# The weights' integer additions and w_out's low-part subtractions, moved from GpSimd to VectorE in an attention and feed-forward kernel

## The chip, the cores and the metric

The kernel runs on one core of one Trainium2 chip. The metric is the device time of one execution in microseconds (us), as the median of several runs. A core has five engines that matter here, each with its own in-order queue of instructions: TensorE (PE in the profile; PEld is its loading of weights), VectorE (DVE), ScalarE (ACT), GpSimd (POOL) and SyncE (SP), which here issues all the transfers (DMA).

## The reference: what is computed

There are two parts. The first is an attention between 512 tokens and 32 state vectors for each of 8 batches and 8 heads of width 64. Both directions are read: tokens attend to the state, and the state attends to the tokens.

```
scores = x @ state^T / 8 ;  a  = softmax over the 32 state vectors ;  xread = a @ state
scores2 = state @ x^T / 8;  a2 = softmax over the 512 tokens       ;  sread = a2 @ x
```

The two results are joined to 8 x 544 = 4352 rows of width 512 (heads side by side). The second part is a feed-forward layer on these rows:

```
h = rows @ w_in      (512 -> 2048)
g = h - tanh(h)
out = g @ w_out      (2048 -> 512)
```

The two weights arrive in 64-bit floating point, the rest in 32-bit.

## The kernel before, in words

**Stages.** The output is made in nine chunks (`Chunk`): eight of 512 token rows, one per batch, and one of 256 rows for the state reads. A chunk runs over 16 hidden blocks `f` of 128 columns. For each block `hidden(f)` makes `h` in PSUM (`hps`), `finish` takes `h - tanh(h)` (`t`, line 383) and splits it in a high and a low part (`g`, lines 90 and 91), and `output(f)` adds three products per 128 rows (lines 413 to 415) into PSUM: high by high, high by low and low by high. The attention weights and the state are folded into `w_in` ahead: `m`, for each chunk and group of four blocks, is the state multiplied with `w_in`.

**Split.** `split(hi, lo, src, sub)` (lines 88 to 91) has ScalarE copy `src` into `hi`, rounded to the reduced 32-bit format that TensorE multiplies fast. Then `lo = src - hi` is made on VectorE, or on the engine given as `sub`.

**Weights.** There are 32 blocks of 128 x 512 in 64-bit form, 16 of each weight. `Weight.load` (line 109) brings one raw block to SBUF, into one of five buffers in turn; each buffer must be free before its next load. `Weight.steps` (lines 118 to 125) makes 32-bit floats of the raw words with integer operations. VectorE shifts and masks the high word (line 120) and puts in the sign and the top exponent bit (line 121). ScalarE makes the rounding increment `r` from the low word (line 123). An integer addition puts the increment on the float's bits (line 124). A block of `w_in` then goes back to DRAM as `wf` and into the state products. A block of `w_out` is converted to a `wor` buffer, of which there are two, and split by `convert_wout` (line 230) into `wo`, which stays in SBUF for all nine chunks.

**Order of the work.** The first steps, from the scores of batch 0 to its first two hidden blocks, follow an order written out by hand, `SEQ` (line 597). Each letter is a step (`a`, `b`, `r`, `p` are the four steps of a weight's conversion), and `keep_in_program_order` pins each step behind the one before on its engine. `firstDVE` is the last VectorE step of this sequence. `FILL` (line 603) says behind which VectorE step the first conversions outside the sequence are queued. All the rest is traced in the loop over chunks and blocks at line 645. There, lists of due steps (`D0`) say at which of the 16 x 9 steps a weight is converted, an attention unit advanced or a state product made. From that trace a planner sets the order of instructions on each engine, with costs of its own; each engine then runs its queue strictly in that order and waits on semaphores.

**Names and lines used below.** `w`: a converted block of `w_in`. `wor`, `wo`: a converted block of `w_out`, and its split parts. `r`: the increment. `m`, `mr`: state products split and raw. `wst`: split blocks of `w_in` for the state products of later batches (lines 178 and 179). `aT`: attention weights, split. `e`, `z`, `s`: softmax values. `sr`: state reads. `mps`, `hps`, `ops`, `sps`: PSUM tiles.

Of the kernel before, what the change touches and what calls it, by code (L numbers as in the profile page):

```python
# [32 lines left out]
def attention_ffn(ctx: ExitStack, tc: tile.TileContext, xT, xn, bd, bh, sp, sm, sl, win, wout, xout, sout):  # L33
# [10 lines left out]
    nc = tc.nc  # L44
# [23 lines left out]
    wo = cpool.tile([P, NFF, 2, DM], F32R, name="wo")  # L68
# [19 lines left out]
    def split(hi, lo, src, sub=None):  # L88

        nc.scalar.copy(hi, src)  # L90
        return (sub or nc.vector).tensor_sub(lo, src, hi)  # L91

    class Weight:
# [17 lines left out]
        def steps(self, dst):  # L111

            if self.src.dtype == F32:
                return [lambda: None] * 3 + [lambda: nc.gpsimd.tensor_copy(dst, self.raw)]
            low, high = self.raw[:, :, 0], self.raw[:, :, 1]
            u, i = dst.bitcast(U32), dst.bitcast(I32)
            r = pool.tile([P, 512], I32, tag="cr", name=f"{self.name}r", bufs=CB)
            return [

                lambda: nc.vector.tensor_scalar(u, high, 3, 0x3FFFFFFF, ALU.logical_shift_left, ALU.bitwise_and),  # L120
                lambda: nc.vector.scalar_tensor_tensor(u, high, 0xC0000000, u, ALU.bitwise_and, ALU.bitwise_or),  # L121

                lambda: nc.scalar.activation(r, low, AF.Copy, scale=2.0**-29),
                lambda: nc.gpsimd.tensor_add(i, i, r),
            ]

        def convert(self, dst):
# [99 lines left out]
    def convert_wout(f, part):  # L227
        w = pool.tile([P, 512], F32, tag="wor", name=f"wor{f}", bufs=RB)
        part.convert(w)
        split(wo[:, f, 0], wo[:, f, 1], w, nc.gpsimd)  # L230


    def attention(b, aT):
# [372 lines left out]
    with tc.issue_after(afters[FILL[0]]):  # L606
        convert_wout(0, wos[0])
    load(1)
    for p in range(2):
# [20 lines left out]
        wo=list(range(0, 15)),  # L630
# [14 lines left out]
    for i in range(B + 1):  # L645
        for f in range(NFF):
            st = 16 * i + f
            with tc.issue_after(first):
                for _ in range(D0["conv"].count(st)):
                    convert_win(*next(convs))  # L650
                    load(1)
                for _ in range(D0["wo"].count(st)):
                    x = next(wo_it)
                    convert_wout(x, wos[x])
                    load(1)
# [73 lines left out]
```

## Time and profile before

| | |
|---|---|
| median of 3 runs | 692.74 us (692.58 to 693.80) |
| the profiled execution | 692.26 us |
| its span, first to last instruction | 690.5 us |
| TensorE busy | 658.9 us (95%) |
| VectorE busy | 462.5 us (67%), 755 instructions |
| ScalarE busy | 378.4 us (55%), 663 instructions |
| GpSimd busy | 78.3 us (11%), 59 instructions |
| moved by DMA | 99.3 MB |

How to read the rows shown below. Times are in us from the start of the span unless marked ns. A group's row names the line, the engine, the operation, the tile written and the tiles read, the shape and the number of instructions; behind the first bar stand busy time in us and the mean of one in ns, behind the second the idle time of the engine just before them and what ended it. A row of single instructions begins with start and length. A wait's row has who waited for whom, the total in us, the number of times and the longest. The slices cut the span in 40 equal parts and give the busy share of each in tenths. VectorE and TensorE instructions in a row overlap slightly at their ends, so a duration is a little longer than the distance to the next start.

### The profile page before, as it was taken

Reading aid. Unit: us, or ns where it says so; the run is one execution under the profiler, and the core shown is the slowest. Engines: PE = TensorE matmul, PEld = TensorE weight load, DVE = VectorE, ACT = ScalarE, POOL = GpSimd, SP = SyncE. Lnnn points to the kernel's source line nnn. Section 1 sums busy time; section 2 is a strip of 40 time slices with the busy share of each in tenths; the row PEclk is TensorE's granted clock in tenths of the full one; section 3 lists DMA queues with packets and bytes.
Section 4 is the critical chain, followed back from the end, with each engine's and each line's share of the span. In section 5 each row is a group of like instructions: output and inputs, shape, how many; then the busy total and the mean of one; then the engine's idle time right before and its main releaser. Section 6 shows DMA issues by size and latency. Waiting matters only on the chain.

```text
span 690.5 us, 9315 instructions
## 1 busy us (share of the span) xinstructions
PE 658.9 (95%) x3386; PEld 520.4 (75%) x3386; DVE 462.5 (67%) x755; ACT 378.4 (55%) x663; POOL 78.3 (11%) x59
## 2 busy tenths in 40 slices
PE   5888996999999999999999999999999999999997
PEld 2455664788788887888788878887878788888896
DVE  5998899965597559556877568636864587434442
ACT  3876867566675665447656555634533354333342
POOL 3676656200000000000000000000000000000000
PEclk9999999999999999999999999999999999999999
DMA  8898763563554553355535522643251312001300
GB/s 289 292 302 289 228 252 118 173 224 97 148 187 144 170 163 123 101 145 152 188 122 180 156 96 92 210 155 126 71 175 31 123 60 91 32 6 46 133 31 30
DMA packets 46317, 99.30 MB, mean 144 GB/s; under 512 B 6208, under 2 KB 12096, under 8 KB 46272
## 3 DMA queue, kind: packets, MB, share of 16 engines
q1 hardware_dynamic: 46272, 98.72, 44.3%
q8 instruction: 26, 0.43, 0.3%
q14 instruction: 19, 0.16, 0.1%
HBM read 66.72 MB, written 31.98 MB: 143 GB/s over the span
## 4 chain that ended last, share of the span: by engine, by line
PE 82%; DVE 9%; ACT 4%; DMA 2%; issue 2%; POOL 1%; SPq 0%; ACTq 0%; POOLq 0%; DVEq 0%
PE ops L415 16%; PE ops L413 16%; PE ops L414 16%; PE hps L376 9%; PE hps L377 9%; PE hps L375 9%; PE mps L187 2%; DVE w L121 2%; PE sps L262 1%; PE rps L329 1%; PE mps L186 1%; PE pps L319 1%; DVE g L91 1%; DVE wor L120 1%; DMA wo4d<-in_wout 1%
## 5 line engine op out<-in xcount | busy, mean ns | idle before, releaser
L413 PE MATMUL ops<-wo,g 128*128 128x512 f32 x544 | 210.2, 396 | 5.1 <-ACT wo L90 3.2
L414 PE MATMUL ops<-wo,g 128*128 128x512 f32 x544 | 214.0, 393 | 0.5 <-POOL wo L91 0.5
L415 PE MATMUL ops<-wo,g 128*128 128x512 f32 x544 | 205.2, 391 | 0.0
L383 DVE TENSOR_TENSOR t<-hps,t 128x512 f32<-128x512 f32 (+1 forms) x142 | 93.1, 658 | 104.4 <-ACT t L383 103.4
L383 ACT ACTIVATE t<-hps 128x512 f32<-128x512 f32 (+1 forms) x142 | 81.2, 574 | 137.7 <-PE hps L377 137.0
L413 PEld LDWEIGHTS ops<-wo,g 128*128 128x128 f32 x544 | 102.3, 188 | 33.7 <-ACT wo L90 5.7
L90 ACT CAST g<-t 128x512 fp32r<-128x512 f32 (+1 forms) x142 | 84.6, 596 | 76.7 <-DVE t L383 69.1
L91 DVE TENSOR_TENSOR g<-t,g 128x512 fp32r<-128x512 f32 (+1 forms) x142 | 99.0, 698 | 40.1 <-ACT g L90 38.6
L415 PEld LDWEIGHTS ops<-wo,g 128*128 128x128 f32 x544 | 102.4, 189 | 23.7 <-issue 1.3
L414 PEld LDWEIGHTS ops<-wo,g 128*128 128x128 f32 x544 | 102.5, 188 | 23.4 <-POOL wo L91 1.4
L375 PE MATMUL hps<-aT,m 128*128 128x512 f32 x248 | 99.3, 401 | 3.6 <-ACT m L90 1.9
L377 PE MATMUL hps<-aT,m 128*128 128x512 f32 x248 | 97.3, 394 | 1.1 <-DVE m L91 1.1
L376 PE MATMUL hps<-aT,m 128*128 128x512 f32 x248 | 98.1, 395 | 0.0
L375 PEld LDWEIGHTS hps<-aT,m 128*128 128x128 f32 x248 | 47.2, 190 | 15.8 <-ACT m L90 3.2
L91 DVE TENSOR_TENSOR wst<-w,wst 64x512 fp32r<-64x512 f32 x64 | 47.0, 734 | 16.9 <-ACT wst L90 15.4
L377 PEld LDWEIGHTS hps<-aT,m 128*128 128x128 f32 x248 | 47.1, 190 | 12.6 <-DVE m L91 2.8
L376 PEld LDWEIGHTS hps<-aT,m 128*128 128x128 f32 x248 | 47.3, 191 | 10.7 <-issue 1.1
L91 DVE TENSOR_TENSOR m<-mr,m 128x1024 fp32r<-128x1024 f32 x31 | 40.9, 1321 | 10.8 <-ACT m L90 10.0
L188 ACT COPY st<-mps 128x512 f32<-128x512 f32 x64 | 36.6, 588 | 13.5 <-PE mps L187 12.8
L90 ACT CAST wst<-w 64x512 fp32r<-64x512 f32 x64 | 39.6, 619 | 2.3 <-issue 1.5
L90 ACT CAST m<-mr 128x1024 fp32r<-128x1024 f32 x31 | 32.3, 1042 | 4.8 <-DMA mr<-md 4.7
L91 POOL TENSOR_TENSOR wo<-wor,wo 128x512 fp32r<-128x512 f32 x16 | 25.2, 1581 | 4.9 <-ACT wo L90 4.8
(218 smaller groups left out, 642.3 us busy)
## 6 DMA issues: line engine op xcount, KB each, us to landing
md<-st SPq DMA_DIRECT2D x144, 128.0 KB, 2.2
mr<-md SPq DMA_DIRECT2D x28, 512.0 KB, 4.1
xT<-in_xT SPq DMA_DIRECT2D x16, 512.0 KB, 4.3
xn<-in_xn SPq DMA_DIRECT2D x16, 512.0 KB, 4.6
w<-wf SPq DMA_DIRECT2D x16, 512.0 KB, 4.6
out_x<-ob SPq DMA_DIRECT2D x32, 256.0 KB, 2.1
wn<-wf SPq DMA_DIRECT2D x8, 512.0 KB, 4.0
ml<-md SPq DMA_DIRECT2D x8, 512.0 KB, 3.6
```

Of the source, the lines that this page charges most:

```text
L90: nc.scalar.copy(hi, src)
L91: return (sub or nc.vector).tensor_sub(lo, src, hi)
L121: lambda: nc.vector.scalar_tensor_tensor(u, high, 0xC0000000, u, ALU.bitwise_and, ALU.bitwise_or),
L187: nc.tensor.matmul(ps, s[:, 0, h], t[:, e], start=(g == 1), stop=True)
L188: nc.scalar.copy(stage[:, e], ps)
L375: nc.tensor.matmul(ps, mhi[k][:, cols], ahi[:, k], start=(k == 0), stop=False)
L376: nc.tensor.matmul(ps, mhi[k][:, cols], alo[:, k], start=False, stop=False)
L377: nc.tensor.matmul(ps, mlo[k][:, cols], ahi[:, k], start=False, stop=(k == nk - 1))
L383: tanhs.append((nc.scalar.activation(t, ps, AF.Tanh).ins, nc.vector.tensor_sub(t, ps, t).ins))
L413: nc.tensor.matmul(o, g[:, 0, tok], wo[:, f, 0], start=(f == 0), stop=False)
L414: nc.tensor.matmul(o, g[:, 0, tok], wo[:, f, 1], start=False, stop=False)
L415: return nc.tensor.matmul(o, g[:, 1, tok], wo[:, f, 0], start=False, stop=(f == NFF - 1)).ins
```

## The change

Two edits. In `Weight.steps` the integer addition of the rounding increment is issued on VectorE instead of GpSimd, for all 32 weight blocks; this includes the four additions `p0` to `p3` of the hand-written sequence, which thereby become VectorE steps of it. In `convert_wout` the subtraction for the low part of `w_out` is issued on VectorE, the default of `split`, instead of GpSimd, for all 16 blocks. Both are traced at the same places as before; the planner sets the order anew. GpSimd keeps two subtractions of the first softmax (line 528), the two of `aT` for batch 0 (line 301), and the constants at the start.

```diff
                 lambda: nc.scalar.activation(r, low, AF.Copy, scale=2.0**-29),
-                lambda: nc.gpsimd.tensor_add(i, i, r),
+                lambda: nc.vector.tensor_add(i, i, r),
             ]
...
     def convert_wout(f, part):
         w = pool.tile([P, 512], F32, tag="wor", name=f"wor{f}", bufs=RB)
         part.convert(w)
-        split(wo[:, f, 0], wo[:, f, 1], w, nc.gpsimd)
+        split(wo[:, f, 0], wo[:, f, 1], w)
```

## The prediction

> **What bounds the kernel now.** I read three views in this order: the busy shares with the slices, a table of busy time over five stretches, and the chain of waits.
>
> ```profile
> PE 658.9 (95%) x3386; PEld 520.4 (75%) x3386; DVE 462.5 (67%) x755; ACT 378.4 (55%) x663; POOL 78.3 (11%) x59
> ...
> PE   5888996999999999999999999999999999999997
> ...
> DVE  5998899965597559556877568636864587434442
> ...
> POOL 3676656200000000000000000000000000000000
> ```
>
> GpSimd (POOL) works only in the first eight of forty slices, the first 138 us. The change can act directly only there. The stretches, whose columns are length, busy time and instructions of PE, PEld, DVE, ACT and POOL, clock, DMA share and GB/s:
>
> ```profile
> 9.00:52.00 43.00, 33.67 (x142) 21.78 (x141) 41.72 (x64) 31.59 (x58) 29.55 (x21) 0.96 0.93 300
> 52.00:122.00 70.00, 56.86 (x229) 38.52 (x228) 63.94 (x84) 48.71 (x84) 44.25 (x30) 0.98 0.63 219
> 122.00:138.00 16.00, 16.00 (x87) 12.74 (x88) 15.63 (x28) 9.44 (x17) 3.33 (x2) 0.89 0.57 178
> 138.00:690.50 552.50, 548.78 (x2927) 446.62 (x2925) 340.31 (x581) 286.82 (x503) 0.00 (x0) 1.00 0.38 119
> ```
>
> From 122 us TensorE is busy without a gap: what remains from there is TensorE's own work, and the change doesn't touch it. Before that TensorE idles, 9.3 us in the second stretch and 13.1 us in the third. So the time can move only by as much as the point where TensorE fills up moves. What decides that point is VectorE: busy 41.7 of 43 us and 63.9 of 70 us, the fullest engine in both. From 9 to 52 us the DMA engines are nearly full too (0.93), with the weights coming in. The chain of waits agrees: VectorE has 9% of it (62 us), second to TensorE, and GpSimd 1%, with pieces such as these (start, length, what):
>
> ```profile
> PE 82%; DVE 9%; ACT 4%; DMA 2%; issue 2%; POOL 1%; SPq 0%; ACTq 0%; POOLq 0%; DVEq 0%
> ...
> 80.94 1.30 POOL wor L124
> 82.24 1.71 POOL wo L91
> ...
> 110.78 1.68 POOL wor L124
> 112.46 2.23 POOL wo L91
> ```
>
> **The change, part by part.** Removed from GpSimd: 32 integer additions (line 124, one per 128x512 block of both weights) and 16 subtractions into `wo` (line 91). Added to VectorE: the same 48. No DMA, no ScalarE step and no matmul is added or dropped.
>
> *What they cost on VectorE.* No integer addition runs on VectorE in this trace. The nearest row is line 121, also two 32-bit integer inputs in SBUF:
>
> ```profile
> 50.24 0.68 DVE L121 SCALAR_TENSOR_TENSOR w<-w22d,w 128x512 uint32<-128x512 uint32 x1
> 50.84 0.68 DVE L121 SCALAR_TENSOR_TENSOR w<-w23d,w 128x512 uint32<-128x512 uint32 x1
> ...
> 53.65 0.41 DVE L120 TENSOR_SCALAR wor<-wo3d 128x512 uint32<-128x512 uint32 x1
> ...
> 58.30 1.67 DVE L121 SCALAR_TENSOR_TENSOR w<-w30d,w 128x512 uint32<-128x512 uint32 x1
> ```
>
> One lasts 0.68 us, but the next starts after 0.60 us, so 0.60 us is what one takes of a full queue: 48 x 0.60 = 28.8 us. The bounds are 0.60 us, if it overlaps its neighbours as here, and 0.69 us, if it never does; I take 0.60, because the queue is full.
>
> [...]
>
> *What they stop costing.* The last row above is the same operation as the first, but 1.67 us long. At that moment GpSimd was running:
>
> ```profile
> 57.93 1.48 POOL L91 TENSOR_TENSOR wo<-wor,wo 128x512 fp32r<-128x512 f32 x1
> 59.37 1.75 POOL L124 TENSOR_TENSOR wor<-wor,wo4r 128x512 int32<-128x512 int32 x1
> ```
>
> So a VectorE instruction with two inputs in SBUF (line 120 too) stands still while a GpSimd addition runs. Groups of VectorE show how much. First from 52 to 140 us, then after 140 us, where GpSimd does nothing (last columns: busy us, mean ns):
>
> ```profile
> L91 DVE TENSOR_TENSOR g<-t,g 128x512 fp32r<-128x512 f32 x13 | 13.6, 1049 | 1.9 <-ACT g L90 1.8
> L383 DVE TENSOR_TENSOR t<-hps,t 128x512 f32<-128x512 f32 x14 | 9.5, 685 | 1.6 <-ACT t L383 1.4
> L91 DVE TENSOR_TENSOR m<-mr,m 128x1024 fp32r<-128x1024 f32 x5 | 9.1, 1828 | 0.5 <-ACT m L90 0.5
> L91 DVE TENSOR_TENSOR wst<-w,wst 64x512 fp32r<-64x512 f32 x8 | 8.5, 1068 | 0.3
> L292 DVE TENSOR_TENSOR e<-e,z 128x512 f32<-128x512 f32 x2 | 2.1, 1063 | 0.0
> ```
>
> ```profile
> L91 DVE TENSOR_TENSOR wst<-w,wst 64x512 fp32r<-64x512 f32 x56 | 38.4, 686 | 16.7 <-ACT wst L90 15.4
> L91 DVE TENSOR_TENSOR m<-mr,m 128x1024 fp32r<-128x1024 f32 x26 | 31.8, 1223 | 10.4 <-ACT m L90 9.6 <-PE ops L413 0.2 <-PE mps L187 0.2
> ```
>
> Line 383, one of whose inputs lies in PSUM, keeps its 685 ns; the others are stretched. Lines 120 and 121, 0 to 52 us and 52 to 140 us, in that order for each line (VectorE busy, count):
>
> ```profile
> 0.00:52.00 52.00, 14.46 (x15) 0.97 0.91 295
> 52.00:140.00 88.00, 11.01 (x17) 0.96 0.62 214
> ```
>
> ```profile
> 0.00:52.00 52.00, 11.82 (x15) 0.97 0.91 295
> 52.00:140.00 88.00, 16.68 (x17) 0.96 0.62 214
> ```
>
> From 52 us on, the stretch above the undisturbed length is: line 120, 11.01 - 17 x 0.41 = 4.0; line 121, 16.68 - 17 x 0.68 = 5.1; `g`, 13 x (1.049 - 0.685) = 4.7; `m`, 5 x (1.828 - 1.223) = 3.0; `wst`, 8 x (1.068 - 0.686) = 3.1; `e`, 2 x (1.063 - 0.685) = 0.8. Sum 20.7 us. Of the 48 moved instructions 31 fall into this stretch (the GpSimd rows number 32 there, and one of them starts before it): 31 x 0.60 = 18.6 us. VectorE gains 2.1 us.
>
> Before 52 us: line 120, 14.46 - 15 x 0.41 = 8.3; line 121, 11.82 - 15 x 0.68 = 1.6; sum 9.9 us. The remaining 17 moved instructions cost 10.2 us. Four GpSimd subtractions stay there (two at line 528, two into `aT`) and keep part of the stretch. I cost this stretch at nothing: the two sums nearly cancel, and the DMA share of 0.93 would hide a small gain. If that cover is missing, it costs the difference of 0.3 us and 1.0 us (1.67 - 0.68) for each instruction that those four still stretch.
>
> *Waits that go and come.* VectorE now waits for GpSimd, and GpSimd for ScalarE:
>
> ```profile
> DVE g L91 <- ACT g L90: 1.8, 2, 1.1
> DVE wor L120 <- POOL wo L91: 1.8, 2, 1.2
> ...
> POOL wo L91 <- ACT wo L90: 4.8, 5, 2.4
> POOL wor L124 <- ACT wo5r L123: 4.3, 1, 4.3
> ```
>
> The wait for `wo` (a `wor` buffer not yet free) ends, since writer and reader are then one engine in order: -1.8 us. New on VectorE are the waits that GpSimd took alone: the addition needs ScalarE's `r`, the subtraction ScalarE's `wo` high part. Whatever is queued behind them waits as well: `t`, `g`, `m`, and behind those TensorE. The nearest row is `g`, with the same pattern of cast and subtraction: 1.8 us for 13. The 13 `wo` subtractions from 52 us on should cost as much, +1.8 us; the additions I cost at nothing, as `r` depends on the load alone and can be ready before line 121 is. Bounds: nothing, if the order places both late enough, and 4.8 + 4.3 = 9.1 us, all of what GpSimd waited.
>
> *The hand-written order.* Four additions (`p0` to `p3`) now stand in VectorE's own start sequence; each delays what follows it there by 0.60 us. `p3` becomes the last VectorE step there, and so the one behind which the second block of `w_in`'s next column group is queued: one 0.60 us step later. These are inside the 17 above.
>
> **Sum.** The profiled execution took 692.26 us around a span of 690.5, 0.5 us below the median of 692.74. 692.26 - 2.1 - 1.8 + 1.8 = 690.2 us.
>
> **The rivals.**
>
> *In-order waits (slower).* The planner sets VectorE's order from its own costs; where ScalarE is later than planned, VectorE stands still with everything behind it. For: ScalarE is busy 48.7 of 70 us, and GpSimd's long waits were for it. Against: VectorE waits for ScalarE for only 3.7 us there today (`g` 1.8, `t` 1.4, `m` 0.5 in the groups). At the bound: 692.3 - 2.1 - 1.8 + 9.1 = 697.5 us. It decides from 3.9 us of new waits on; up to there they are paid for.
>
> *Nothing moves.* DMA and ScalarE set the pace as soon as VectorE eases: 692.3 us. For: 0.93 DMA share early. Against: 0.63 from 52 us on.
>
> *Shorter path.* The pieces of GpSimd in the chain, 1.30 + 1.71 + 1.68 + 2.23 = 6.9 us, become 4 x 0.60 = 2.4 and no wait comes new: a further -4.5 us, with the 2.1 of VectorE 685.7 us. Against: behind VectorE's queue the steps start later than on an idle GpSimd.
>
> *Pure load (slower).* If the stretching had another cause than GpSimd, 18.6 us would be added to a full VectorE after 52 us: 692.3 + 18.6 = 710.9 us. Against: the rows at 50 and 58 us. [...]
>
> **How the numbers follow.** What this kernel's measurement can tell from no change is about 0.2%, 1.4 us. The forecast gets 0.48, and its own range is 688.4 (no new waits) to 693.0 us (0.69 for each of 31: +2.8); of that 0.37 lies below 690.9 us and 0.11 within 0.2%. In-order waits 0.32, nothing moves 0.08, shorter path 0.09, pure load 0.03. Faster 0.37 + 0.09 = 0.46; same 0.11 + 0.08 = 0.19; slower 0.32 + 0.03 = 0.35. The range runs from just under the shorter path, 685.0, to the bound of the waits, 697.5; pure load and what little lies outside are left out.
>
> **What would show it.** Right: lines 120, 121, `g`, `m` and `wst` before 140 us at 0.41, 0.68, 0.69, 1.22 and 0.69 us; line 124 on VectorE at 0.68 with 0.60 from start to start; TensorE full a few us before 122. Wrong: VectorE idle before 122 us that grew by over 4 us with ScalarE as releaser (in-order waits), an unmoved 52 to 122 stretch with less busy VectorE (nothing moves), or stretched rows beside an idle GpSimd (pure load). A difference that arises after 138 us would be none of these, and would mean that the planner's order changed there.

## The result, and the profile after

The changed kernel takes 688.78 us (median of 6 runs, 687.84 to 690.70), the kernel before beside it 693.44 us. The ratio is 0.9939 with a 95% interval from 0.9922 to 0.9956: by the ratio 4.2 us faster (the two medians lie 4.7 us apart). The forecast was 690.2 us, 2.1 us faster than the profiled execution, with a range of its own from 688.4 to 693.0 us. So the direction was right, the forecast gain was half of the measured one, and 688.78 us lies just inside the lower end of that range. The profiled execution took 688.88 us around a span of 687.1 us, against 692.26 around 690.5: 3.4 us less.

The changed kernel's busy times, slices and, last, its chain of waits:

```profile
PE 660.5 (96%) x3386; PEld 521.7 (76%) x3386; DVE 458.2 (67%) x803; ACT 377.9 (55%) x663; POOL 6.6 (1%) x11
...
PE   4788988999999999999999999999999999999997
...
DVE  5897999965695559556876568546853587434442
...
POOL 2100000000000000000000000000000000000000
...
PE 85%; DMA 6%; DVE 4%; ACT 3%; issue 1%; SPq 0%; ACTq 0%; DVEq 0%
```

VectorE has 48 instructions more (803 against 755) and is busy 4.3 us less (458.2 against 462.5). GpSimd's part fell from 78.3 to 6.6 us. In the chain of waits VectorE's share fell from 9% to 4%, and DMA's rose from 2% to 6%. The table of stretches for the changed kernel, with the same columns as before:

```profile
9.00:52.00 43.00, 31.81 (x126) 19.21 (x126) 38.95 (x78) 28.92 (x54) 5.43 (x4) 0.92 0.89 289
52.00:122.00 70.00, 63.42 (x248) 44.87 (x249) 64.75 (x119) 52.11 (x90) 0.00 (x0) 0.93 0.68 235
122.00:138.00 16.00, 16.00 (x95) 13.11 (x95) 15.47 (x30) 11.87 (x22) 0.00 (x0) 1.00 0.63 198
```

TensorE's idle time from 52 to 122 us fell from 13.1 to 6.6 us, while from 9 to 52 us it rose from 9.3 to 11.2 us. Over the whole span it fell by 5.0 us, from 31.6 to 26.6 us, while TensorE's busy time rose by 1.6 us (its mean granted clock was 0.988, against 0.993 before): 3.4 us in all. Its last pause before it fills up ended at 121.9 us before, behind a VectorE queue, and ends at 112.2 us now (single TensorE instructions, first of the kernel before, then of the changed one):

```profile
121.88 0.65 PE L186 MATMUL mps<-wst,sms 128*128 128x512 f32 x1 [3.64 <-DVE sr L335]
```

```profile
112.19 0.80 PE L414 MATMUL ops<-wo,g 128*128 128x512 f32 x1 [1.27 <-DVE wo L91]
```

In the profile of a second execution of the changed kernel (`e6_both_again` below) the last pause of over 1 us ends at 114.1 us, and two short ones of 0.45 and 0.48 us follow, at 123.1 and 138.3 us.

The stretched groups are back at their undisturbed lengths. From 52 to 140 us in the changed kernel:

```profile
L91 DVE TENSOR_TENSOR g<-t,g 128x512 fp32r<-128x512 f32 x14 | 9.6, 685 | 0.1
L91 DVE TENSOR_TENSOR wo<-wor,wo 128x512 fp32r<-128x512 f32 x13 | 8.9, 684 | 0.1
L91 DVE TENSOR_TENSOR m<-mr,m 128x1024 fp32r<-128x1024 f32 x6 | 7.3, 1214 | 0.0
L91 DVE TENSOR_TENSOR wst<-w,wst 64x512 fp32r<-64x512 f32 x8 | 5.5, 687 | 0.3
```

`g` fell from 1049 to 685 ns, `m` from 1828 to 1214, `wst` from 1068 to 687. The added integer additions, and one of the line-121 instructions beside them:

```profile
34.52 0.69 DVE L124 CUSTOM_DVE_ANT_0 w<-w,w11r 128x1024 uint16<-128x1024 uint16 x1
35.12 0.68 DVE L124 CUSTOM_DVE_ANT_0 w<-w,w10r 128x1024 uint16<-128x1024 uint16 x1
35.72 0.69 DVE L121 SCALAR_TENSOR_TENSOR wor<-wo1d,wor 128x512 uint32<-128x512 uint32 x1
```

They last 0.68 to 0.69 us and follow each other after 0.60 us, as costed. What VectorE waits for from 52 to 122 us has changed:

```profile
DVE wor L120 <- DMA wo4d<-in_wout: 1.1, 1, 1.1
DVE w L120 <- DMA w31d<-in_win: 1.1, 1, 1.1
DVE w L120 <- PE mps L149: 1.0, 1, 1.0
DVE z L289 <- ACT e L282: 0.8, 1, 0.8
DVE wor L120 <- DMA wo5d<-in_wout: 0.6, 1, 0.6
DVE w L120 <- DMA wf<-w: 0.3, 1, 0.3
```

It now waits for loads (2.8 us here) and for a block's way back to DRAM (0.3 us). It doesn't wait for ScalarE before any `wo` subtraction.

### The profile page after: what moved, and what is told of

Same layout as the page of the kernel before. It is cut to its first block, busy times and chain, and to the rows that moved or that the text cites. A ratio compares the mean times of both kernels' runs of the same rounds, so it can differ in the third digit from the quotient of the medians.

```text
span 687.1 us, 9286 instructions
## 1 busy us (share of the span) xinstructions
PE 660.5 (96%) x3386; PEld 521.7 (76%) x3386; DVE 458.2 (67%) x803; ACT 377.9 (55%) x663; POOL 6.6 (1%) x11
## 4 chain that ended last, share of the span: by engine, by line
PE 85%; DMA 6%; DVE 4%; ACT 3%; issue 1%; SPq 0%; ACTq 0%; DVEq 0%
PE ops L413 17%; PE ops L414 17%; PE ops L415 17%; PE hps L376 9%; PE hps L377 9%; PE hps L375 9%; PE mps L187 2%; PE sps L262 1%; PE rps L329 1%; DMA mr<-md 1%; PE mps L186 1%; DMA w01d<-in_win 1%; DMA wf<-w 1%; PE pps L319 1%; DMA w31d<-in_win 1%; DMA wo1d<-in_wout 1%
## 5 line engine op out<-in xcount | busy, mean ns | idle before, releaser
L91 DVE TENSOR_TENSOR g<-t,g 128x512 fp32r<-128x512 f32 (+1 forms) x142 | 93.3, 657 | 42.4 <-ACT g L90 41.1
L377 PEld LDWEIGHTS hps<-aT,m 128*128 128x128 f32 x248 | 46.7, 188 | 11.0 <-DVE m L91 1.0
L91 DVE TENSOR_TENSOR wst<-w,wst 64x512 fp32r<-64x512 f32 x64 | 43.9, 686 | 16.4 <-ACT wst L90 15.0
L375 PEld LDWEIGHTS hps<-aT,m 128*128 128x128 f32 x248 | 46.6, 188 | 10.5 <-issue 0.7
L376 PEld LDWEIGHTS hps<-aT,m 128*128 128x128 f32 x248 | 46.7, 188 | 10.0 <-issue 0.5
L91 DVE TENSOR_TENSOR m<-mr,m 128x1024 fp32r<-128x1024 f32 x31 | 37.8, 1220 | 9.3 <-ACT m L90 8.6
L188 ACT COPY st<-mps 128x512 f32<-128x512 f32 x64 | 36.7, 587 | 12.3 <-PE mps L187 12.0
L187 PE MATMUL mps<-wst,sms 128*128 128x512 f32 x64 | 24.7, 394 | 0.0
```

Source lines behind the costliest of these rows:

```text
L187: nc.tensor.matmul(ps, s[:, 0, h], t[:, e], start=(g == 1), stop=True)
L188: nc.scalar.copy(stage[:, e], ps)
L375: nc.tensor.matmul(ps, mhi[k][:, cols], ahi[:, k], start=(k == 0), stop=False)
L376: nc.tensor.matmul(ps, mhi[k][:, cols], alo[:, k], start=False, stop=False)
L377: nc.tensor.matmul(ps, mlo[k][:, cols], ahi[:, k], start=False, stop=(k == nk - 1))
```

## The experiments

Three theories were to be told apart. Relief: GpSimd instructions hold up VectorE's, VectorE sets the pace until TensorE fills up, and the gain is the stretch removed less the work added. Path: the way from a load to a ready block got shorter. Order: the planner's new order made the gain.

**Parts of the change.** `e1_adds_only` moves the 32 additions alone, `e2_subs_only` the 16 subtractions alone.

```diff
 e1_adds_only, against the changed kernel
-        split(wo[:, f, 0], wo[:, f, 1], w)
+        split(wo[:, f, 0], wo[:, f, 1], w, nc.gpsimd)
 e2_subs_only, against the changed kernel
-                lambda: nc.vector.tensor_add(i, i, r),
+                lambda: nc.gpsimd.tensor_add(i, i, r),
```

> Only the 32 integer additions move to VectorE; the 16 w_out subtractions stay on GpSimd. Relief (a GpSimd instruction that reads SBUF holds up VectorE's two-input and line-120 instructions, and the gain is that stretch minus the load): two thirds of the whole change, VectorE's total busy time falls by about 3 us and the time to about 690.5 us. Path (the gain is the shorter way from load to wo, whatever VectorE's stretch): the additions stand in all 32 conversions, the subtractions only in 16, so again about two thirds, but VectorE's busy time plays no part. Order (the planner's new order makes the gain): no rule, anything from 687 to 694 us.

> Only the 16 w_out subtractions move to VectorE; the 32 additions stay on GpSimd. Relief: one third of the whole change, VectorE's total busy time falls by about 1.5 us, the time to about 692 us. Path: the subtraction is the last step before TensorE can use a block, and GpSimd took 1.28 to 2.25 us for it against 0.68 us, so it should give at least half of the whole, 691 us or less. Order: anything from 687 to 694 us.

`e1_adds_only`: 688.44 us, ratio 0.9939 (0.9922 to 0.9956), VectorE busy 459.9 us. `e2_subs_only`: 687.17 us, ratio 0.9915 (0.9902 to 0.9928), VectorE busy 458.5 us. The expectation of two thirds and one third fell: each part alone gives as much as both together, or more. VectorE's totals show part of why. The additions alone take 2.6 us off VectorE (462.5 to 459.9; about 3 was expected), the subtractions alone 4.0 us (to 458.5; about 1.5 was expected), and both together only 4.3 us (to 458.2). So the parts don't add: on top of the subtractions the additions take 0.3 us, on top of the additions the subtractions take 1.7 us. In time each part alone gained more than it took off VectorE, 4.5 us for 2.6 and 5.8 us for 4.0; this pair doesn't explain that.

**Contention alone.** `e3_idle_pool_work` gives GpSimd 48 additions back that nobody waits for. All other engines have the same instructions in the same order as in the changed kernel.

```diff
         split(wo[:, f, 0], wo[:, f, 1], w)
+        for _ in range(3):
+            nc.gpsimd.tensor_add(spare, wo[:, f, 0].bitcast(F32), wo[:, f, 0].bitcast(F32))
```

> The changed kernel with 48 more 128x512 additions on GpSimd (three per w_out block, each reading the block's high part twice, written to a spare tile that nobody reads). No other engine waits for them, and the order of every other engine is that of the changed kernel, so only contention can act. Relief: lines 120 and 121, the additions, g, m, wst and the wo subtractions on VectorE stretch again to 1.2 to 1.8 us where they meet one, 48 times about 0.7 us or some 30 us on an engine that is already full from 22 to 122 us, and the time rises by 10 to 30 us, to 699 to 719 us. Path and order: 688.8 us as before, nothing but GpSimd busy.

Measured: 711.10 us, ratio 1.0262 (1.0249 to 1.0275), so 22.3 us more than the changed kernel. VectorE's busy time rose by 27.6 us to 485.8 us. Its groups from 52 to 140 us, and the added GpSimd group (line 92 is line 91 of the other kernels, since a line was added):

```profile
L92 DVE TENSOR_TENSOR wo<-wor,wo 128x512 fp32r<-128x512 f32 x11 | 11.5, 1042 | 0.0
L92 DVE TENSOR_TENSOR g<-t,g 128x512 fp32r<-128x512 f32 x10 | 9.4, 940 | 0.0
L386 DVE TENSOR_TENSOR t<-hps,t 128x512 f32<-128x512 f32 x12 | 8.2, 681 | 0.1
```

```profile
L233 POOL TENSOR_TENSOR spare<-wo 128x512 f32<-128x512 f32 x48 | 65.6, 1367 | 75.7 <-ACT wo L91 73.2
```

The instructions with two inputs in SBUF are stretched again, and `t`, with one input in PSUM, is not. Path and order can't act here, so the contention is shown, and its price in this run: 0.58 us of VectorE for each GpSimd addition (27.6 us for 48).

**Does VectorE set the pace?** `e4_no_adds` drops the additions from the changed kernel.

```diff
-                lambda: nc.vector.tensor_add(i, i, r),
+                lambda: None,
```

> The changed kernel without the 32 integer additions (the weights miss the rounding increment of their low word; ScalarE still makes it). It takes 32 x 0.60 = 19.2 us from VectorE between 12 and 135 us and nothing from elsewhere. If VectorE sets the pace before TensorE fills up (the prediction's reading): 3 to 10 us less than the changed kernel, 679 to 686 us, bounded by TensorE's 13 us of idle time between 22 and 122 us. If the loads or ScalarE take over as soon as VectorE eases: 688 us, with VectorE idle for about 19 us more.

Measured: 674.54 us, ratio 0.9737 (0.9725 to 0.9750), 14.2 us less than the changed kernel, more than the upper end expected. VectorE's busy time fell by 18.4 us to 439.8 us, so each us off VectorE was worth 0.77 us. The run also prices the additions on either engine. With them on VectorE its total is 18.4 us higher (458.2), with them on GpSimd 18.7 us higher (458.5, `e2_subs_only`). With the subtractions on VectorE it is the same for VectorE whether it makes an addition itself or is held up by one. TensorE's busy time fell by 8.1 us too; the last section says what that may be.

**Once more side by side, and two variants.** `e6_both_again` is the changed kernel, `e7_subs_again` is `e2_subs_only`, both unaltered. `e5_no_pool` also moves the last four GpSimd subtractions. `e8_same_fill` queues one conversion behind the same VectorE step as before the change.

```diff
 e5_no_pool, against the changed kernel
-    P0 = json.loads('[0, 0, 0, 0, 1]')
+    P0 = json.loads('[0, 0, 0, 0, 0]')
-    SEQ = 'S0 c0 T0 S1 D D M0 c1 q0 a0 ... M1 b0 q1 E1 ...'
+    SEQ = 'S0 c0 T0 S1 D D M0 c1 B0 a0 ... M1 b0 B1 E1 ...'
 e8_same_fill, against the changed kernel
-    afters = [firstDVE[0], tanhs[0][1], tanhs[1][1]]
+    afters = [tanhs[1][1], tanhs[0][1], tanhs[1][1]]
```

> The changed kernel once more, beside the next three on one chip. Theory after the first four runs: up to about 122 us the time follows VectorE's busy time, about 0.8 us for each us (48 GpSimd additions that held it up for 27.6 us cost 22 us; 19.2 us less work on it gave 14 us), and the planner's order adds a few us either way. Expected 688 to 689 us.

> Only the 16 subtractions on VectorE, beside the changed kernel. VectorE's busy total was 458.5 us in that run against 458.2 us with both parts moved, so by VectorE's time the two are equal within 0.3 us; any difference beyond about 1 us is then the order or the path. Theory (the additions cost VectorE on either engine about the same): 687 to 689 us, within 1.5 us of the changed kernel. Rival (the first run's 687.2 against 688.8 was a real advantage of leaving the additions on GpSimd): 1 to 2 us below the changed kernel again.

> The changed kernel with the last four GpSimd subtractions (two of the first softmax at line 528, two into aT for batch 0) on VectorE as well: GpSimd only sets constants. By VectorE's time: 4 x 0.60 = 2.4 us more work, against some 2 us of stretch that ends: 0 to 1 us either way, 688 to 690 us. By the path: the first softmax is the start of everything, and its two subtractions take 0.68 us instead of 1.18 and 1.42 us, 0.5 to 1 us sooner: 687.5 us. If the order decides: 686 to 691 us.

> The changed kernel, but the second block of w_in's next column group queues behind the same VectorE step as before the change (the second hidden block's subtraction), not behind the addition p3 that has become the last step of the hand-written start. This undoes the one side effect of the change on the traced order. If that queueing matters by itself: up to 0.6 us less. Otherwise it is a measure of what a small change of the planner's input does: 687 to 691 us, with nothing that VectorE's total would explain.

| | VectorE busy, us | median, us | ratio (95% interval) |
|---|---|---|---|
| `e6_both_again` | 458.7 | 689.50 | 0.9943 (0.9924 to 0.9962) |
| `e7_subs_again` | 458.4 | 687.06 | 0.9915 (0.9899 to 0.9931) |
| `e5_no_pool` | 457.8 | 686.33 | 0.9900 (0.9883 to 0.9917) |
| `e8_same_fill` | 457.9 | 688.50 | 0.9931 (0.9916 to 0.9947) |

The advantage of leaving the additions on GpSimd came again, 2.4 us here and 1.6 us in the first pair, with VectorE totals 0.3 us apart. The intervals of the two ratios overlap a little, so I call it likely, and its cause open. `e5_no_pool` is the fastest kernel that computes everything, 6.6 us below the kernel before (692.95 us beside it). It lies 3.2 us below the changed kernel beside it, more than the expectation by VectorE's time (688 to 690 us) or by the path (687.5 us) gave. VectorE's total is only 0.9 us lower. Only the range named for the order, 686 to 691 us, holds it; the cause of the rest is open. The changed place in the order (`e8_same_fill`) makes no difference that can be told from none.

**Early, late, and writes without reads.** `e11_early_work` and `e12_late_work` put 21 idle GpSimd additions into the changed kernel, early or late. `e9_pool_writes` puts in 48 fills that write and don't read. TensorE, VectorE and ScalarE keep the order of the changed kernel in all three.

```diff
 e11_early_work, against e3_idle_pool_work
-        for _ in range(3):
+        for _ in range(7 if f < 3 else 0):
 e12_late_work, against e3_idle_pool_work
-        for _ in range(3):
+        for _ in range(3 if f >= 9 else 0):
 e9_pool_writes, against the changed kernel
+        for _ in range(3):
+            nc.gpsimd.tensor_copy(spare[:, 0:1], wo[:, f, 0, 0:1].bitcast(F32))
+            nc.gpsimd.memset(spare, 0.0)
```

> The changed kernel with 21 extra GpSimd additions that nobody waits for, seven behind each of the w_out blocks 0 to 2, so between about 31 and 58 us; every other engine keeps its order. They should hold up VectorE for some 12 us (48 of them did for 27.6 us). If the transfers set the pace before 52 us, as the prediction had it when it costed that stretch at nothing: under 3 us more than the changed kernel, below 692 us. If VectorE sets the pace there too: about 0.8 us for each, some 9 us more, 697 to 699 us.

> The same with 21 extra GpSimd additions, three behind each of the w_out blocks 9 to 15, so between about 102 and 140 us. If VectorE sets the pace up to the point where TensorE fills up: about 9 us more than the changed kernel, 696 to 699 us. If TensorE has work enough of its own by then: under 3 us more.

> The changed kernel with 48 GpSimd fills (constant 0.0 into a spare tile of 128x1280, three behind each w_out block, each behind a one-element copy), which write but don't read; every other engine keeps its order. If it is GpSimd's reading that collides with VectorE's second input: the two-input instructions (line 121, the additions, g, m, wst, wo) keep 0.68 us (m 1.22), only line 120, which reads and writes fast, may stretch, VectorE's total grows by less than 8 us, the time to 689 to 695 us. If any GpSimd work does: as with the 48 additions, VectorE's total up by over 20 us, and 705 to 711 us.

`e11_early_work`: 701.13 us, ratio 1.0115 (1.0095 to 1.0134), VectorE 471.5 us. That is 13.3 us more on VectorE and 12.3 us more time. `e12_late_work`: 701.94 us, ratio 1.0135 (1.0112 to 1.0158), VectorE 473.2 us: 15.0 us more on it, 13.2 us more time. Both are 2 to 6 us above the times expected; the additions held up VectorE for more than the 12 us assumed. In `e11_early_work` 12 of the 21 additions start before 52 us, the others up to 64 us (shortest, median and longest in ns, then the first and the last start in us):

```profile
L233 POOL TENSOR_TENSOR spare<-wo x21: 1038/1367/2639, 30.2 to 64.0; 128x512 f32<-128x512 f32 x21
```

An estimate: at 13.3 / 21 = 0.63 us each, the 12 early ones are 7.6 us of the stretch and the others 5.7 us. If the transfers hid the early part, the time could have risen by 5.7 us at most; it rose by 12.3 us. So VectorE sets the pace before 52 us as well as after; the transfers don't hide it. The share of the DMA engines from 9 to 52 us fell with it, from 0.89 in the changed kernel to 0.79: there the transfers wait for VectorE, at least in part.

`e9_pool_writes`: 691.66 us, ratio 0.9985 (0.9972 to 0.9999), VectorE 464.6 us. That is 6.4 us more on VectorE than in the changed kernel and 2.9 us more time, less for each us than in the other runs. Its VectorE groups from 52 to 140 us (line 92 is line 91 before, and line 121 is line 120):

```profile
L92 DVE TENSOR_TENSOR wo<-wor,wo 128x512 fp32r<-128x512 f32 x13 | 8.9, 683 | 0.1
L92 DVE TENSOR_TENSOR g<-t,g 128x512 fp32r<-128x512 f32 x13 | 8.9, 682 | 0.1
...
L121 DVE TENSOR_SCALAR w<-w33d 128x512 uint32<-128x512 uint32 x1 | 1.5, 1470 | 0.0
```

```profile
L234 POOL MEMSET spare<- 128x1280 f32 x48 | 57.2, 1191 | 2.9
```

GpSimd is nearly as busy as with the additions (57.2 us of fills against 65.6 us of additions), but from 52 us on the two-input instructions keep their 0.68 us: `wo` takes 683 and `g` 682 ns here, 1042 and 940 ns beside the additions of `e3_idle_pool_work`. The shift-and-mask of line 120 alone is stretched there: 12.71 us for 19 of them, 0.67 us each, against 6.85 us for 17, 0.40 us each, in the changed kernel. So in these two runs the additions, which read SBUF, stretched the two-input instructions, and the fills, which only write, did not. Why the fills stretch line 120, which has one input, no row says.

**A version that might beat all.** `e10_pool_adds_only` has the additions on GpSimd and all subtractions on VectorE.

```diff
 e10_pool_adds_only, against e5_no_pool
-                lambda: nc.vector.tensor_add(i, i, r),
+                lambda: nc.gpsimd.tensor_add(i, i, r),
```

> A version that might beat all: the 32 additions stay on GpSimd, every subtraction goes to VectorE (the 16 of w_out, two of the first softmax, two into aT). If the additions cost VectorE the same on either engine and the four early subtractions gave the 3 us that lie between the run without GpSimd work and the changed kernel: 685 to 687 us. If they gave it only because GpSimd then had nothing at all to do: 687 to 689 us.

Measured: 693.92 us, ratio 1.0014 (1.0002 to 1.0027): no faster than the kernel before, and both expectations missed. VectorE's total is 464.0 us, 5.6 us above `e7_subs_again`. Four moved subtractions account for 2.4 us of that; the rest is stretch from another meeting of the two engines' queues. The profile has it after 52 us: from there to 140 us line 121 takes 16.13 us for 19 instructions (12.26 us for 17 in `e7_subs_again`) and a subtraction of `m` 1.63 us (1.21 us). TensorE waits 5.5 us for `wo` subtractions on VectorE, 1.4 us in `e7_subs_again`. Why the planner's order came out so wasn't tried.

All different kernels together, by VectorE's busy time (where a kernel was measured twice, its first measurement):

| | VectorE busy, us | median, us |
|---|---|---|
| `e4_no_adds` | 439.8 | 674.54 |
| `e5_no_pool` | 457.8 | 686.33 |
| `e8_same_fill` | 457.9 | 688.50 |
| the changed kernel | 458.2 | 688.78 |
| `e2_subs_only` | 458.5 | 687.17 |
| `e1_adds_only` | 459.9 | 688.44 |
| before | 462.5 | 692.96 |
| `e10_pool_adds_only` | 464.0 | 693.92 |
| `e9_pool_writes` | 464.6 | 691.66 |
| `e11_early_work` | 471.5 | 701.13 |
| `e12_late_work` | 473.2 | 701.94 |
| `e3_idle_pool_work` | 485.8 | 711.10 |

From the first row to the last it is 36.6 us for 46.0 us, 0.80 us for each us of VectorE. The rows lie within about 2.6 us of that line. In the runs where only GpSimd's idle work differs, VectorE's part is shown to be the cause. What puts a kernel 2 to 3 us off the line stays open: a new order is the obvious candidate, but `e9_pool_writes`, whose order is unchanged, lies 2.6 us below it too. For the change itself this means: its 4.3 us of VectorE are worth 3.4 us by the line, and the measured 4.2 us can't be told from that, nor from 2 us more or less by path or order. No run has the changed work in the old order.

## Why the prediction was right, and where it was not

*What bounds the kernel*: right about VectorE; `e3_idle_pool_work` and `e4_no_adds` show that the time follows it in both directions. The measure it named, the point where TensorE fills up, was not right. In the changed kernel's profile that point moved by 9.7 us, the span by 3.4 us. And in `e7_subs_again`, which is faster than the changed kernel, TensorE's last pause of over 0.5 us ends later than in the kernel before:

```profile
135.62 0.50 PE L375 MATMUL hps<-aT,m 128*128 128x512 f32 x1 [1.02 <-DVE t L383]
```

The span is TensorE's busy time, 659 to 661 us in these three, and its idle time in sum: 31.6 us before, 26.6 us in the changed kernel, 25.8 us in `e7_subs_again`.

*The cost on VectorE*: nearly right. It took 0.60 us each; `e4_no_adds` gives 18.4 us for 32, so 0.575 us each. This held although the addition turned out to be another kind of instruction than the row it was priced by.

*The stretch that ends*: right in kind, and each named group came back to the length it was given. It was too small in sum: VectorE was to gain 2.1 us and gained 4.3. The term most at fault is the stretch before 52 us, costed at nothing; the lower price of an addition is the other part (48 x 0.025 = 1.2 us, if the subtractions cost the same). Two things were wrong in the term. The sum of two lines, 9.9 us, left out the groups beside them. In the trace of before, these three carry 2 x (1.218 - 0.685) + 2 x (1.204 - 0.685) + (2.287 - 1.223) = 3.2 us more up to 52 us:

```profile
L576 DVE TENSOR_TENSOR g<-t,g 128x512 fp32r<-128x512 f32 x2 | 2.4, 1218 | 0.0
L91 DVE TENSOR_TENSOR g<-t,g 128x512 fp32r<-128x512 f32 x2 | 2.4, 1204 | 0.1
L91 DVE TENSOR_TENSOR m<-mr,m 128x1024 fp32r<-128x1024 f32 x1 | 2.3, 2287 | 0.0
```

Against that stands what the four remaining GpSimd subtractions still stretch, for instance one line-121 instruction of 1.75 us and one addition of 1.31 us in the changed kernel. And the cover named for the term isn't there: the DMA share of 0.93 was read as a limit, while in `e11_early_work` time rose by 12.3 us for 13.3 us of VectorE, over half of them in that stretch.

*Waits that go and come*: half right. The wait for a free `wor` buffer went. The 1.8 us of new waits for ScalarE before the `wo` subtractions did not come. An addition did wait for ScalarE's `r`, once, for 0.9 us before 52 us; that had been costed at nothing. In their place came waits for loads, 2.8 us from 52 to 122 us and 2.2 us before 52 us for one block of `w_out` alone. VectorE's idle time from 9 to 122 us rose from 7.3 to 9.3 us, so the net of this step was 2 us of loss where nothing was forecast. The upper bound of 9.1 us, called all of what GpSimd waited, was not all: its waits for ScalarE from 52 to 140 us sum to 14.9 us.

*The sum*: with both measured terms in it, 692.3 - 4.3 + 2.0 = 690.0 us, as good as the forecast of 690.2 us and 1.1 us above the profiled 688.88. So the two misses nearly cancel in the sum; that it came no further off than it did is in part luck, and the 1.1 us that VectorE's account leaves over is not explained.

*The rivals*: in-order waits for ScalarE stayed far below the 3.9 us from which they decide. The shorter path doesn't decide: `e3_idle_pool_work` keeps the changed kernel's path and is slower than the kernel before by 18 us. Whether the path gave a part of the 4.2 us was not measured. Pure load is refuted by the rows above, but its other half is true: a us more on VectorE does cost 0.8 us.

*The hand-written order*: the step that moved with `p3` costs nothing that can be told (`e8_same_fill`). The prediction calls the block that is queued behind it the second of `w_in`'s next column group; by the kernel it is the first, `w10`.

*Two parts in one sum*: the prediction priced 48 moved instructions alike. They are not alike, and their prices depend on what else GpSimd does. With the subtractions on VectorE, an addition on GpSimd costs VectorE what making it costs, 18.7 against 18.4 us for 32 (0.58 us each); with the subtractions on GpSimd it costs 2.6 us more than that in sum, 0.66 us each. A subtraction on GpSimd costs more in both cases: 4.0 us (additions on GpSimd) or 1.7 us (additions on VectorE) above the 16 x 0.60 = 9.6 us of making them, 0.85 or 0.71 us each. So the gain on VectorE is for the larger part that of the subtractions, but no fixed share of it belongs to either.

## What to carry to other kernels

GpSimd instructions that read SBUF beside a full VectorE were not free here: they cost VectorE 0.58 to 0.85 us each, as much as VectorE needs to do the same work (0.58 to 0.60 us) or more, so the account is made by summing the stretch of VectorE's groups against the same groups where GpSimd is idle, all groups and all stretches. The high DMA share before 52 us (0.93 before the change, 0.89 after) was no proof that a gain is hidden; what starts the transfers may be the same engine (the share fell to 0.79 when VectorE was held up in `e11_early_work`), and a few idle instructions on another engine price that in one run. When a planner orders the work, a version that looks better by parts (`e10_pool_adds_only`) has to be run: here it came out 7 to 9 us above what its parts had promised.

## What the runs showed of the hardware that was not expected

On VectorE the 32-bit integer addition stands in the trace of the changed kernel as a custom instruction on 128x1024 of `uint16`. It takes 0.68 to 0.69 us, no longer than a plain two-input instruction on 128x512 (0.69 us for line 121 beside it).

In the trace of before, TensorE lost more around two pauses than their length. After these pauses of 1.64 and 1.58 us close together, matmuls start 0.43 us apart, and only from 74.8 us on 0.23 us apart. The granted clock shows it: 1.00 up to 70 us, 0.50 from 72 to 74 us (single instructions, then stretches of 2 us with the columns of the stretches above):

```profile
68.46 1.13 PE L149 MATMUL mps<-w,sps 128*128 128x512 f32 x2 [1.64 <-ACT st L152]
71.17 0.79 PE L375 MATMUL hps<-aT,m 128*128 128x512 f32 x1 [1.58 <-ACT m L90]
71.76 0.63 PE L376 MATMUL hps<-aT,m 128*128 128x512 f32 x1
72.19 0.63 PE L375 MATMUL hps<-aT,m 128*128 128x512 f32 x1
...
74.82 0.39 PE L375 MATMUL hps<-aT,m 128*128 128x512 f32 x1
75.04 0.39 PE L376 MATMUL hps<-aT,m 128*128 128x512 f32 x1
```

```profile
68.00:70.00 2.00, 1.13 (x2) 0.30 (x2) 1.89 (x4) 1.95 (x4) 0.00 (x0) 1.00 0.22 49
70.00:72.00 2.00, 0.83 (x2) 0.73 (x3) 1.54 (x3) 1.78 (x4) 1.56 (x1) 0.72 0.74 279
72.00:74.00 2.00, 2.00 (x6) 1.27 (x6) 2.00 (x2) 1.95 (x4) 1.45 (x1) 0.50 0.73 262
74.00:76.00 2.00, 2.00 (x10) 1.68 (x9) 2.00 (x4) 1.69 (x4) 1.15 (x2) 0.93 0.42 84
```

From 71.17 us to the start at 74.82 us nine matmuls take 3.65 us; at 0.23 us each it would be 2.1 us, so by this estimate 1.6 us were lost. All nine are on split tiles. On plain 32-bit tiles matmuls of this size start 0.43 us apart at a clock of 1.00 too (the eight of line 373, 27.8 to 30.8 us). That the pauses brought the clock down is my reading of this one place; no run tested it. `e4_no_adds`, with less TensorE idle time (18.9 us), has 652.4 us of TensorE busy time for the same matmuls, against 660.5 us in the changed kernel. Its mean granted clock is 1.000 against 0.988, and 0.012 x 687 us gives 8.2 us, as an estimate of what the lower clock took. That fits the difference of 8.1 us, so that slow stretches like this one make it up is likely, but it wasn't tested by itself; if so, they are more than half of the 14.2 us that the run gained.
